# Decay attention and two feed-forward layers on one core: a fourth score tile in the late units' ring, and weight scales from column squares and products of ones

## The chip, the core and the metric

The kernel runs on one NeuronCore of a Trainium2 chip. The metric is the device time of one execution in microseconds (us). The core has five engines that run side by side and wait for each other through semaphores: TensorE (PE in the rows; its weight loads are PEld), VectorE (DVE), ScalarE (ACT), GpSimd (POOL) and SyncE (SP), whose queue issues the transfers here. Each takes its own instructions strictly in the order in which the program holds them.

## The reference

Attention with a decay, then two feed-forward layers over all 2304 tokens:

```
scores = q @ k.T / 8 + (cum[i] - cum[j]), causal      # 4 batches, 8 heads, 576 tokens, head size 64
x = softmax(scores) @ v                               # 2304 x 512
x = relu(x @ w_in) ** 2 @ w_out                       # 512 -> 2048 -> 512
g = x @ w_gate;  x = (silu(g) * (x @ w_val)) @ moe2_w_out   # 512 -> 1536 -> 512
```

`cum` is the running sum of log(f). Inputs and output are float32.

## The kernel before, in words

Most products are made three times in f16, with a high and a low part of each operand (hi*hi, hi*lo, lo*hi), so each f32 weight must be turned into two f16 tiles with a power-of-two scale, and that scale has to be known before the split.

**The plan.** The code doesn't issue instructions as it goes. Each piece of work is a step that `add` puts into a `Plan` with an engine, an estimated duration, the steps it depends on, the buffer rings it takes and uses, and a priority. `Plan.order` walks through time with these estimates, gives each free engine its ready step of the lowest priority number whose rings have room, and so fixes the order of every engine's instructions once and for all. On the chip an engine never passes over a step that is not ready. The tables of numbers at the top (`GPRI`, `EPRI`, `VPRI`, `IPRI`, `ILOAD`, `OPRI`, `OLOAD`, lines 167 to 173) are priorities of the early attention units, of V, and of the loads and steps of the weights.

**Fillers.** Exactly 130 steps `keep_clock` (line 295), each a 128x512 product of ones with itself into a bank that nobody reads, have the worst priority of all. The planner puts one wherever TensorE has nothing else that is ready and a bank of the ring `hp` is free; so where they stand in the order tells where the plan saw a hole on TensorE. All 130 are issued, in every case.

**Stages.** The attention is cut into 32 units: 16 early ones (tokens 0 to 255 of a batch and a pair of heads) and 16 late ones (tokens 256 to 575). `attn_unit` builds one. For each tile of 128 queries of a late unit TensorE makes the scores (line 817; for the 64 left-over tokens of both heads `tail_scores`, line 826, with the block tile `BOTH` that `corner` fills on POOL, line 767); DVE adds the decay into a score tile `s` (line 856), ACT takes the exponential (876) and the high part `p` (935), DVE the low part (939), SP transposes p by DMA (963), and TensorE mixes with V (`mix`, line 995). A late unit's Q is loaded to `qr` (722), rounded by ACT into the high part (737), and POOL makes the low part from both (740), which frees `qr`; `kr` likewise. Beside the attention TensorE works through the first feed-forward layer in token tiles of 256 (`mlp_pair`, lines 1193 and 1263); what is left of it follows the attention, and then comes the second layer in five rounds (`mlp2`, lines 1459 and 1575), each of which begins by finding a scale of its own input (line 1337 on TensorE).

**Scales of the weights.** `stage` loads a unit of 512 columns or rows of a weight in two or three pieces and joins the words; `extent` (line 417, DVE) takes the largest magnitude of each of the 128 partitions, one column of the table `MT` for each piece. `scale_of` calls `top`: TensorE turns the columns against an identity (line 326, `turn`), DVE takes the largest along the row (330) and squares it (332), TensorE spreads it with a product of ones (335, `spread`), and DVE makes the power of two (`power`, lines 305 to 311). Units 1 and 2 of gate and value are looked at early: `peek` loads them once for the extent alone (1078, 1084), ACT rescales (1099), and DVE shifts (1103) and copies into `MT` (1104); then the same `scale_of`. The four units of W_in take their extent from a Gram product instead.

Of the kernel before, what the change touches and what calls it, by code (L numbers as in the profile page):

```python
# [8 lines left out]
F32 = mybir.dt.float32  # L9
F32R = mybir.dt.float32r  # L10
F16 = mybir.dt.float16
BF16 = mybir.dt.bfloat16
I32 = mybir.dt.int32
# [150 lines left out]
    return 0.1 + n * 0.0021  # L164


GPRI = 866
GATE0 = -1
GATE = 5
EPRI = [394, 178, 220, -430, -80, -72, -882, -468, 406, -704, 233, 411, 552, 339, -276, -947]  # L170
VPRI = [84, 242, 446, 595]
IPRI, ILOAD = [-317, 915, 396, 320], [-195, 548, 99, 663]
OPRI, OLOAD = [368, 413, 378, 287], [27, -1147, 442, -1239]
VERBOSE = False
WHOLE = 2
SQUARE = 7
# [7 lines left out]
def decay_attention_moe_kernel(ctx: ExitStack, tc, q, k, v, f, w1, w2, wg, wv, wo, outT):  # L184
# [61 lines left out]
    XI, XS = table("xi", B + 1), table("xs", B + 1)  # L246
    KX = table("kx", 2, B * NP)
    FY = table("fy", B + 1)
    MT = table("mt", 2 * NG1 + 9 * NG2 + 4 * NG1, dt=BF16)
    NSC = 2 * NG1 + 3 * NG2  # L250
    SWI, SWS = table("swi", NSC), table("sws", NSC)
    ISF, ISG, ISV = (SWI[:, 2 * NG1 + NG2 * n : 2 * NG1 + NG2 * n + NG2] for n in range(3))
# [67 lines left out]
    def top(col, n, deps, pri, then, us, square=False, where="hp"):  # L320
        c = {}
        buf, alloc = bank(where)

        def turn():
            c["ps"] = alloc()
            nc.tensor.matmul(c["ps"][0:n, 0:P], col(), ident, start=True, stop=True)

        def largest():
            c["r"] = r = small.tile([P, 1], BF16, tag="top", bufs=4, name="top")
            nc.vector.tensor_reduce(r[0:n], c["ps"][0:n, 0:P], axis=mybir.AxisListType.X, op=ALU.max)  # L330
            if square:
                nc.vector.tensor_tensor(r[0:n], r[0:n], r[0:n], op=ALU.mult)

        def spread():
            nc.tensor.matmul(c["ps"][:, P : P + 1], ones[0:n, :], c["r"][0:n], start=True, stop=True)

        a = add(PE, 0.25, turn, [*deps, ready0], pri, take=[buf])
        r_buf = Buf("top", 4)
        a = add(DVE, 0.3 + (0.17 if square else 0), largest, [a], pri, take=[r_buf], use=[buf])
        a = add(PE, 0.15, spread, [a], pri, use=[buf, r_buf])  # L340
        return add(DVE, us, lambda: then(c["ps"][:, P : P + 1]), [a], pri, use=[buf])
# [17 lines left out]
    def stage(nm, u, places, pri, lpri, deps=(), gates=(), where="hp"):  # L359
# [55 lines left out]

        def extent(piece, at):
            nc.vector.tensor_reduce(
                MT[:, at : at + 1], piece["hi"].bitcast(F32), axis=mybir.AxisListType.X, op=ALU.max,
                apply_absolute_value=True,
            )  # L420

# [19 lines left out]
    def scale_of(nm, u, c, pri, where="hp"):  # L441
        idx = COL[nm] + u
        kk, mask = (13, 0x7F000000) if nm == "o" else (13 if nm in "gv" else 14, 0x7F800000)
        lo, hi = c["cols"]
        whole = 1 if nm == "i" else 512
        return top(
            lambda: MT[:, lo:hi], hi - lo, c["stat"], pri,
            lambda ps: power(ps, VSCALE * 1.02 * whole, kk, SWI[:, idx : idx + 1], SWS[:, idx : idx + 1], mask), 0.9,
            where=where, square=whole > 1,
        )  # L450

    def split(c, idx, slot, scaled):
        key, pri = c["key"], c["pri"]
# [226 lines left out]
    def attn_unit(idx, b, pr, half, opened):  # L680
# [34 lines left out]
        def raw_tile(name, w):  # L715
            if early:
                return h0.tile([P, SPLIT], F32, tag="qk", bufs=QKN, name=name)
            return pools["at"].tile([P, w], F32, tag=name, bufs=2, name=name)

        def load_q():  # L720
            c["qr"] = raw_tile("qr", QW)[:, :qn]
# [24 lines left out]
        def k_lo():  # L746
            nc.gpsimd.tensor_tensor(c["K"][:, 1], c["kr"], c["K"][:, 0].bitcast(F32), op=ALU.subtract)

        kr, qr = (Buf("qk", QKN), Buf("qk", QKN)) if early else (Buf("kr", 2), Buf("qr", 2))
        bias = kq_buf("bias")  # L750
        KA, QA = (kr, qr) if early else (kq_buf("KA"), kq_buf("Q"))
        lk = take(SP, DMA_ISSUE, load_k, [], [kr], nbytes=P * 4 * kmax)
# [3 lines left out]
        if not early:  # L756
            kh = take(ACT, act_us(kmax), k_hi, [lk], [KA], use=[kr])
            kl = add(POOL, pool_us(kmax), k_lo, [kh], pri, use=[KA, kr])
            qh = take(ACT, act_us(qn), q_hi, [lq], [QA], use=[qr])
            ql = add(POOL, pool_us(qn), q_lo, [qh], pri, use=[QA, qr])  # L760
            ready = [kh, kl, qh, ql]
            both = Buf("both%d" % (idx % 2), 1)

            def corner(h):
                def copy():
                    r = slice(64 * h, 64 * h + 64)
                    nc.gpsimd.tensor_copy(BOTH[idx % 2][r, :, r], c["Q"][r, :, QW - 64 : QW])

                return copy

            b0 = take(POOL, 0.44, corner(0), [qh, ql], [both], use=[QA])
            b1 = add(POOL, 0.44, corner(1), [qh, ql], pri, use=[QA, both], order=[b0])
            tail_ready = [kh, kl, b0, b1]
# [8 lines left out]
        for ti, i in enumerate(tiles):  # L782
# [9 lines left out]
            ng = heads[1][5] + 1  # L792
            cuts = [(0, ext if early else max(ext, 256))] if ext <= 512 else [(0, ext // 2), (ext // 2, ext)]
            cg_buf = Buf("cg", 6)
            sbufs = [Buf(tg + "s", SN if early else 3) for _ in range(ng)]
            masks = []
            for h, r0, r1, qc, M, g in heads:

# [9 lines left out]
            for ci, (n0, n1) in enumerate(cuts):  # L808
# [13 lines left out]
                def tail_scores(cuts=cuts, ti=ti):  # L822
                    for cc, (m0, m1) in enumerate(cuts):
                        c["ps", ti, cc, 0] = c["ps", ti, cc, 1] = at_tile()
                        for qi, ki in ((0, 0), (0, 1), (1, 0)):
                            nc.tensor.matmul(
                                c["ps", ti, cc, 0][:, : m1 - m0], BOTH[idx % 2][:, qi], c["K"][:, ki, m0:m1],
                                start=(qi, ki) == (0, 0), stop=qi == 1,
                            )

# [15 lines left out]
                for (h, r0, r1, _, _, g), mk, pbuf in zip(heads, masks, pbufs):  # L846
                    new = ci == 0 and (h == 0 or g == 1)

                    def soft(st=st, g=g, h=h, r0=r0, r1=r1, n0=n0, n1=n1, ti=ti, ci=ci, ext=ext, new=new):
                        if new:  # L850
                            st["s", g] = pool().tile([P, kw], F32, tag="s", bufs=SN if early else 3, name="s")
                            if g == 0:
                                st["cg"] = small.tile([P, 2, 4], F32, tag="cg", bufs=6, name="cg")
                        s, cg = st["s", g], st["cg"][:, g]
                        e1 = min(n1, ext)
                        nc.vector.tensor_tensor_reduce(  # L856
                            out=s[r0:r1, n0:e1], in0=c["ps", ti, ci, h][r0:r1, : e1 - n0],
                            in1=c["bias"][r0:r1, h, n0:e1],
                            scale=-0.125, scalar=3.0e38 if ci == 0 else cg[r0:r1, 0:1],
                            op0=ALU.add, op1=ALU.min, accum_out=cg[r0:r1, ci : ci + 1],  # L860
                        )
# [206 lines left out]
    def peek(nm, u, places):  # L1068
# [31 lines left out]

        def shift():
            t = cell["t"][:, : len(places)].bitcast(I32)
            nc.vector.tensor_scalar(t, t, 3, None, op0=ALU.logical_shift_left)
            nc.vector.tensor_copy(MT[:, m0 : m0 + len(places)], cell["t"][:, : len(places)])

        a = add(ACT, 0.3, real, [stats[-1][0]], GPRI, use=[t_buf])
        a = add(DVE, 0.35, shift, [a], GPRI, use=[t_buf])
# [539 lines left out]
    def open_half():  # L1647
# [4 lines left out]
        for n in range(2):  # L1652
# [123 lines left out]
```

## Time and profile before

| | before |
|---|---|
| median of 3 runs | 956.47 us (956.20 to 956.74) |
| the profiled execution | 959.76 us |
| its span, first to last instruction | 958.1 us |
| busy: PE, PEld | 944.1, 738.1 us |
| busy: DVE, ACT, POOL | 627.6, 603.4, 326.7 us |
| DMA | 117.46 MB, mean 123 GB/s |

The page cuts the span into 40 slices of some 24 us each. TensorE's digit is 9 in all of them but two 8s, the granted clock's likewise, the 18th slice (from 407 to 431 us) being one of the lower ones. DVE and ACT are at 7 to 9 tenths up to about the 24th slice (575 us) and at 3 to 4 tenths after it. A busy time is a share of the span, not a limit: TensorE's matmuls overlap and their ends are modelled, so how long one takes is read from the start of one to the start of the next.

### The profile page before, as it was taken

To read this page: it belongs to the slowest core of one execution; us is meant where nothing else is said; L and a number is where in the kernel's file an instruction comes from. 1 tells how busy PE (TensorE), PEld (TensorE's weight loads), DVE (VectorE), ACT (ScalarE), POOL (GpSimd) and SP (SyncE) were. 2 spreads that over 40 slices of the span, in tenths; PEclk is the share of its full clock that TensorE was granted. 3 is DMA by queue.
4 is the path that set the end of the run, shared out by engine and by line. 5 is a ranking of instruction groups with operands and counts; after the bars stand their busy time and mean duration, and the time that the engine had idled before them with its cause. 6 is when DMAs were issued, how large, how long until landed. Compare 5 with 4: busy or idle time off the path is not lost.

```text
span 958.1 us, 22457 instructions
## 1 busy us (share of the span) xinstructions
PE 944.1 (99%) x8845; PEld 738.1 (77%) x8845; DVE 627.6 (66%) x1438; ACT 603.4 (63%) x1147; POOL 326.7 (34%) x454
## 2 busy tenths in 40 slices
PE   9999999999999999989999999999999999999998
PEld 3686787888888788867888887778977776877774
DVE  4788888577666878768999898446464363433332
ACT  5899898588787898767978766225343343332332
POOL 1432163545544456333333453131321241110120
PEclk9999999999999999989999999999999999999999
DMA  9797249767979897999835411002020001000101
GB/s 286 229 360 243 42 113 216 224 164 149 182 150 191 176 230 182 241 220 269 204 111 175 156 45 45 2 1 90 1 66 2 2 1 44 2 1 12 34 1 44
DMA packets 147946, 117.46 MB, mean 123 GB/s; under 512 B 98241, under 2 KB 136129, under 8 KB 142593
## 3 DMA queue, kind: packets, MB, share of 16 engines
q1 hardware_dynamic: 147840, 116.04, 47.4%
q8 instruction: 69, 1.13, 0.5%
q14 instruction: 37, 0.29, 0.1%
HBM read 83.44 MB, written 9.51 MB: 97 GB/s over the span
## 4 chain that ended last, share of the span: by engine, by line
PE 51%; DVE 2%; issue 0%; ACT 0%; DMA 0%; SPq 0%; DVEq 0%; ACTq 0%
PE acc L1575 14%; PE v L1459 14%; PE h L1459 10%; PE acc L1263 6%; PE h L1193 5%; PE ps L995 1%; DVE r L1476 0%; PE ps L817 0%; DVE s L856 0%; DVE ms L1329 0%; DMA out_dram<-tmp 0%; DVE p L939 0%; DVE tmp L1476 0%; ACT L1497 0%; DVE i L1402 0%
## 5 line engine op out<-in xcount | busy, mean ns | idle before, releaser
L1193 PE MATMUL h<-x,i 128*128 128x256 f16 x1728 | 208.2, 274 | 0.0
L1263 PE MATMUL acc<-g,o 128*128 128x256 f16 x1728 | 207.6, 273 | 0.0
L1193 PEld LDWEIGHTS <-i 128*128 128x128 f16 x1728 | 164.8, 98 | 28.2 <-issue 6.3
L1263 PEld LDWEIGHTS <-o 128*128 128x128 f16 x1728 | 163.8, 98 | 28.1 <-issue 6.5
L1575 PE MATMUL acc<-o,f 128*128 128x512 f16 (+1 forms) x720 | 145.9, 358 | 0.9 <-ACT o L1548 0.5
L1575 PEld LDWEIGHTS <-f 128*128 128x128 f16 x720 | 70.0, 98 | 65.0 <-issue 1.4
L1538 POOL TENSOR_TENSOR tmp<-tmp,o 128x256 f32<-128x256 f32 (+1 forms) x30 | 23.4, 780 | 250.8 <-ACT o L1532 250.8
L1241 POOL TENSOR_TENSOR g<-tmp,g 128x512 f16<-128x512 f32 x56 | 71.5, 1276 | 106.9 <-ACT g L1236 94.9
L801 POOL TENSOR_SCALAR_AFFINE_SELECT bias<-bias 128x128 f32<-128x128 f32 (+1 forms) x160 | 61.6, 394 | 113.6 <-DVE cg L856 62.5
L939 DVE SCALAR_TENSOR_TENSOR p<-s,cg,p 128x512 f16<-128x512 f32 (+4 forms) x112 | 77.0, 702 | 27.7 <-ACT p L935 27.3
L876 ACT ACTIVATE s<-s,cg 128x256 f32<-128x256 f32 (+4 forms) x144 | 83.1, 579 | 17.8 <-DVE cg L856 17.6
L856 DVE CUSTOM_DVE_ANT_0 s<-ps,bias 128x512 f32<-128x512 f32 (+3 forms) x160 | 72.5, 479 | 24.3 <-PE ps L817 16.3
L935 ACT ACTIVATE p<-s,cg 128x512 f16<-128x512 f32 (+4 forms) x112 | 67.7, 615 | 7.7 <-issue 2.5
L1459 PEld LDWEIGHTS <-g 128*128 128x128 f16 x720 | 65.4, 98 | 8.8 <-issue 0.8
L1459 PEld LDWEIGHTS <-v 128*128 128x128 f16 x720 | 65.4, 98 | 6.5
L1504 ACT ACTIVATE r<-r,ms 128x768 f32<-128x768 f32 (+1 forms) x30 | 26.1, 869 | 69.8 <-DVE r L1476 69.7
L1459 PE MATMUL v<-i,g 128*128 128x256 f16 (+1 forms) x540 | 67.9, 262 | 0.4 <-DVE tmp L1476 0.4
L1459 PE MATMUL v<-i,v 128*128 128x256 f16 (+1 forms) x540 | 67.9, 262 | 0.0
L1476 DVE TENSOR_TENSOR r<-r,h 128x512 f32<-128x512 f32 (+1 forms) x30 | 19.0, 633 | 73.9 <-PE h L1459 67.0
L1542 POOL TENSOR_TENSOR r<-r,o 128x768 f32<-128x768 f32 (+1 forms) x30 | 45.8, 1526 | 41.3 <-ACT o L1535 40.5
L1476 DVE TENSOR_TENSOR r<-r,v 128x512 f32<-128x512 f32 (+1 forms) x60 | 38.0, 634 | 32.8 <-PE v L1459 30.6
L1459 PEld LDWEIGHTS <-eg 128*128 128x128 f16 x540 | 49.2, 98 | 8.9
(190 smaller groups left out, 1630.7 us busy)
## 6 DMA issues: line engine op xcount, KB each, us to landing
raw<-in_moe_w_out_dram SPq DMA_DIRECT2D x11, 1024.0 KB, 6.7
bias<-cum_d SPq DMA_DIRECT2D x16, 576.0 KB, 4.9
raw<-in_moe_w_val_dram SPq DMA_DIRECT2D x9, 1024.0 KB, 6.1
raw<-in_moe_w_gate_dram SPq DMA_DIRECT2D x9, 1024.0 KB, 6.8
raw<-in_moe_w_in_dram SPq DMA_DIRECT2D x8, 1024.0 KB, 5.8
vr<-in_v_dram SPq DMA_DIRECT2D x32, 256.0 KB, 4.3
x_d<-tmp SPq DMA_DIRECT2D x18, 256.0 KB, 3.6
kr<-in_k_dram SPq DMA_DIRECT2D x16, 288.0 KB, 4.1
```

The lines of the kernel that those rows point to most:

```text
L801: nc.gpsimd.affine_select(diag, diag, pattern=[[-1, w]], compare_op=ALU.is_ge, fill=-8e9, base=0, channel_multiplier=1)
L856: nc.vector.tensor_tensor_reduce(out=s[r0:r1, n0:e1], in0=c["ps", ti, ci, h][r0:r1, : e1 - n0], in1=c["bias"][r0:r1, h, n0:e1], scale=-0.1 ...
L876: nc.scalar.activation(s[:, :ext], s[:, :ext], AF.Exp, bias=cg[:, mc : mc + 1], scale=-1.0, accum_out=cg[:, 2:3],)
L935: nc.scalar.activation(pv[:, 0, :ext], s[:, :ext], AF.Copy, scale=cg[:, 3:4])
L939: nc.vector.scalar_tensor_tensor(pv[:, 1, :ext], s[:, :ext], cg[:, 3:4], pv[:, 0, :ext], op0=ALU.mult, op1=ALU.subtract,)
L1193: nc.tensor.matmul(HP[key][:, u, :], w[:, wi, kk, c * P : (c + 1) * P], x[:, xi, kk, :], start=(kk == 0 and (wi, xi) == (0, 0)), stop=(kk ...
L1241: lows[2].tensor_tensor(G[k0][1][:, 1], G[k0][0], G[k0][1][:, 0], op=ALU.subtract)
L1263: nc.tensor.matmul(acc[:, d - part[0], :], w[:, wi, c, d * P : (d + 1) * P], G[k0][1][:, gi, u, :], start=(m == 0 and d == part[0] and (wi ...
L1459: nc.tensor.matmul(R[reg][:, which, :w], t[:, wh, w1_ : w1_ + P], x[:, xh, xi, kk], start=fresh and which == 0 and kk == 0 and (wh, xh) == ...
L1476: nc.vector.tensor_tensor(out(), x(), y(), op=ALU.add)
L1542: nc.gpsimd.tensor_tensor(g, g, R["g"][:, 0, 1:4], op=ALU.subtract)
L1575: nc.tensor.matmul(acc_of(d), wd[:, cc, d * P : (d + 1) * P], R["g"][:, gi, 2 * m : 2 * m + 2].rearrange("p a t -> p (a t)"), start=mm == ...
```

## The change

It does four things. The 13 units of W_out, the second layer's output weight, gate and value no longer turn their extents: DVE squares each column of them (new line 458, one instruction for each piece), and TensorE multiplies each square with ones and sums them in one bank (new line 463); the extents stand in a float32 table `ME`, so `peek` needs one shift (1121) and no copy. W_in and V keep `top`. The late units' ring of score tiles has four tiles for three; in exchange `qr` has one buffer for two and `BOTH` one for two. And the tables of priorities have new numbers, which gives every engine another order.

```
-GPRI = 866
+GPRI = 864
-EPRI = [394, 178, 220, -430, -80, -72, -882, -468, 406, -704, 233, 411, 552, 339, -276, -947]
-VPRI = [84, 242, 446, 595]
-IPRI, ILOAD = [-317, 915, 396, 320], [-195, 548, 99, 663]
-OPRI, OLOAD = [368, 413, 378, 287], [27, -1147, 442, -1239]
+EPRI = [244, -200, -7, -648, 65, -536, 142, -686, 364, 99, 136, 548, 546, -423, -309, -1418]
+VPRI = [228, 246, 473, 561]
+IPRI, ILOAD = [-407, 890, 363, 306], [-509, 265, 885, 1236]
+OPRI, OLOAD = [402, 434, 247, 170], [-1221, -130, 84, -1046]
...
-    MT = table("mt", 2 * NG1 + 9 * NG2 + 4 * NG1, dt=BF16)
+    MT, ME = table("mt", NG1, dt=BF16), table("me", 2 * NG1 + 9 * NG2 + 4 * NG1)
...
-        whole = 1 if nm == "i" else 512
-        return top(
-            lambda: MT[:, lo:hi], hi - lo, c["stat"], pri,
-            lambda ps: power(ps, VSCALE * 1.02 * whole, kk, SWI[:, idx : idx + 1], SWS[:, idx : idx + 1], mask), 0.9,
-            where=where, square=whole > 1,
-        )
+        def then(ps, rows=1):
+            power(ps, VSCALE * 1.02 * rows, kk, SWI[:, idx : idx + 1], SWS[:, idx : idx + 1], mask)
+
+        if nm == "i":
+            return top(lambda: MT[:, lo:hi], hi - lo, c["stat"], pri, then, 0.9, where=where)
+        buf, alloc = bank(where)
+        r_buf, t = Buf("top", 4), {}
+
+        def squares():
+            t["r"] = r = small.tile([P, 4], BF16, tag="top", bufs=4, name="top")
+            for n in range(lo, hi):
+                m = ME[:, n : n + 1]
+                nc.vector.tensor_scalar(r[:, n - lo : n - lo + 1], m, m, None, op0=ALU.mult)
+
+        def total():
+            t["ps"] = alloc()
+            for n in range(hi - lo):
+                nc.tensor.matmul(t["ps"][:, 0:1], ones, t["r"][:, n : n + 1], start=n == 0, stop=n == hi - lo - 1)
+
+        a = add(DVE, 0.16 * (hi - lo), squares, c["stat"], pri, take=[r_buf])
+        a = add(PE, 0.1 + 0.06 * (hi - lo), total, [a, ready0], pri, take=[buf], use=[r_buf])
+        return add(DVE, 0.72, lambda: then(t["ps"][:, 0:1], 2), [a], pri, use=[buf])
...
-            return pools["at"].tile([P, w], F32, tag=name, bufs=2, name=name)
+            return pools["at"].tile([P, w], F32, tag=name, bufs=2 if name == "kr" else 1, name=name)
...
-            both = Buf("both%d" % (idx % 2), 1)
+            both = Buf("both%d" % (idx % 1), 1)
...
-            sbufs = [Buf(tg + "s", SN if early else 3) for _ in range(ng)]
+            sbufs = [Buf(tg + "s", SN if early else 4) for _ in range(ng)]
...
-            nc.vector.tensor_scalar(t, t, 3, None, op0=ALU.logical_shift_left)
-            nc.vector.tensor_copy(MT[:, m0 : m0 + len(places)], cell["t"][:, : len(places)])
+            m = ME[:, m0 : m0 + len(places)].bitcast(I32)
+            nc.vector.tensor_scalar(m, t, 3, None, op0=ALU.logical_shift_left)
```

What the order of the instructions shows, at three places. In the changed kernel line numbers above 445 are 17 higher.

TensorE, late in the attention, where the second of the four units that are looked at early (gate, unit 1) gets its scale: before, nine fillers stand between two score steps, and the turn follows at once.

```order
L817 MATMUL ps<-KA,Q 128x384 x6
L295 LDWEIGHTS ones
L295 MATMUL ps<-ones 128x512
...
L826 MATMUL ps<-KA,both 128x288 x6
L326 LDWEIGHTS mt
L326 MATMUL ps<-ident,mt 2x128
L995 LDWEIGHTS VT
```

The same place now; the scale's two products stand after a mix and before a full group of the first layer, and another such group comes before the next score step.

```order
L1012 MATMUL ps<-PT,VT 64x128
L463 LDWEIGHTS ones
L463 MATMUL ps<-top,ones 128x1
L463 LDWEIGHTS ones
L463 MATMUL ps<-top,ones 128x1
L1280 LDWEIGHTS o_1905
L1280 MATMUL acc<-g,o_1905 128x256
...
L834 MATMUL ps<-KA,Q 128x512 x6
```

The nine fillers are gone from here, and no filler stands anywhere in the late attention; up to this place there are 120 of them for 121.

DVE at the same scale, before: between the copy for the turn (1104) and the reduction of the turned row (330) stand ten instructions of the attention.

```order
L1103 TENSOR_SCALAR pk<-pk 128x2
L1104 CAST mt<-pk 128x2
L856 ISA s,cg<-ps,bias 64x288
...
L889 RECIPROCAL cg<-cg 128x2
...
L1025 SCALAR_TENSOR_TENSOR x<-ps,kx,x 128x128
L330 TENSOR_REDUCE top<-ps 2x1
L332 TENSOR_TENSOR top<-top 2x1
```

DVE there now:

```order
L873 ISA s,cg<-ps,bias,cg 64x288
L873 ISA cg 64x1
L1121 TENSOR_SCALAR me<-pk 128x2
L458 TENSOR_SCALAR top<-me 128x1 x2
L956 SCALAR_TENSOR_TENSOR p_7262<-s,cg,p_7262 128x384
```

Shift and squares follow each other, and TensorE waits for DVE once for a scale where it waited twice.

TensorE in the second layer, at the end of the round of the 64-token rests, and at the very end of the program, now; before, no filler stands at either place. Without the fillers, the last 2982 products of the program stand in the same order in both kernels.

```order
L1592 MATMUL acc<-o_11217,f_6520 128x256
L295 LDWEIGHTS ones
L295 MATMUL ps<-ones 128x512
...
L1592 MATMUL acc<-o_11433,f_5649 128x512
L295 LDWEIGHTS ones
L295 MATMUL ps<-ones 128x512
...
L1592 MATMUL acc<-o_13730,f_6520 128x512
L295 LDWEIGHTS ones
L295 MATMUL ps<-ones 128x512
L1789 UNCONDITIONAL_BRANCH
```

Two fillers stand at the first of these spots, five at the second (six products later), and three behind the last product of the program.

## Rows read from the trace of the kernel before

**Rows 1.** Busy time by stretch: span us, busy us (instructions) by engine, clock, DMA, GB/s.
```profile
core 0: us, PE busy (x) PEld busy (x) DVE busy (x) ACT busy (x) POOL busy (x), PEclk, DMA share, GB/s
...
408.40:415.20 6.80, 4.75 (x45) 3.07 (x46) 5.39 (x15) 3.01 (x10) 3.17 (x4) 1.00 1.16 156
415.20:422.00 6.80, 5.44 (x51) 3.40 (x50) 5.40 (x18) 3.59 (x7) 1.47 (x6) 0.50 1.00 320
...
490.00:690.00 200.00, 199.83 (x1940) 168.09 (x1938) 143.17 (x225) 116.46 (x178) 67.35 (x55) 1.00 0.19 62
...
720.00:953.00 233.00, 233.00 (x1730) 168.96 (x1728) 90.18 (x137) 76.58 (x125) 46.15 (x37) 1.00 0.03 11
```

**Rows 2.** Waits of TensorE, whole span: total us, times, longest.
```profile
PE ps L335 <- DVE top L332: 2.5, 4, 1.4
PE ps L326 <- DVE mt L1104: 2.1, 1, 2.1
```

**Rows 3.** TensorE in order of time, 408.9 to 422.6 us: start, duration, what, wait.
```profile
408.97 2.12 PE L295 MATMUL ps<-ones 128*128 128x512 bf16 x9
410.74 1.15 PE L826 MATMUL ps<-KA,both 128*128 128x288 f32 x6
413.95 0.22 PE L326 MATMUL ps<-ident,mt 128*2 128x128 bf16 x1 [2.06 <-DVE mt L1104]
414.09 0.69 PE L995 MATMUL ps<-PT,VT 128*64 128x128 f16 x18
414.72 1.02 PE L1193 MATMUL h<-x,i 128*128 128x256 f16 x6
417.10 0.16 PE L335 MATMUL ps<-top,ones 2*128 2x1 bf16 x1 [1.36 <-DVE top L332]
417.19 1.46 PE L1193 MATMUL h<-x,i 128*128 128x256 f16 x6
```

**Rows 4.** DVE in order of time, the same place.
```profile
409.68 1.22 DVE L1084 TENSOR_REDUCE pk<-raw 128x1 f32<-128x1024 f32 x1 [1.95 <-DMA raw<-in_moe_w_gate_dram]
...
413.72 0.17 DVE L1104 CAST mt<-pk 128x2 bf16<-128x2 f32 x1
...
416.59 0.27 DVE L330 TENSOR_REDUCE top<-ps 2x1 bf16<-2x128 f32 x1
416.90 0.15 DVE L332 TENSOR_TENSOR top<-top 2x1 bf16<-2x1 bf16 x1
```

**Rows 5.** TensorE in order of time: a 4-column product of ones, and what follows.
```profile
546.18 0.17 PE L1337 MATMUL ps<-sq,ones 128*128 128x4 bf16 x1
546.21 1.47 PE L1263 MATMUL acc<-g,o 128*128 128x256 f16 x12
```

**Rows 6.** TensorE in order of time where the second layer's third round begins to accumulate.
```profile
710.58 1.24 PE L1575 MATMUL acc<-o,f 128*128 128x512 f16 x5 [0.48 <-ACT o L1548]
712.22 1.46 PE L1575 MATMUL acc<-o,f 128*128 128x512 f16 x6 [0.39 <-DVE tmp L1606]
```

**Rows 7.** The program's end, in order of time: last products, last eviction.
```profile
952.23 1.46 PE L1575 MATMUL acc<-o,f 128*128 128x512 f16 x6
...
954.36 0.48 DVE L1606 TENSOR_SCALAR o<-acc,ms 128x256 f32<-128x256 f32 x1 [2.41 <-ACT o L1604]
```

**Rows 8.** Loads of Q (line 722): issue to landing; POOL frees a buffer; ACT's next cast.
```profile
DMA to landing us min/median/max: 2.1/3.4/9.3
...
361.36 0.87 POOL L740 TENSOR_TENSOR Q<-qr,Q 128x320 fp32r<-128x320 f32 x1
...
373.92 0.45 ACT L737 CAST Q<-qr 128x320 fp32r<-128x320 f32 x1
```

**Rows 9.** Loads of the peeks (line 1078): issue to landing; the DMA queue, 300 to 480 us.
```profile
DMA to landing us min/median/max: 5.8/6.9/8.5
...
q1 hardware_dynamic: 60023, 38.61, 94.1%
```

**Rows 10.** Busy time by stretch (columns as in rows 1), where weights are split.
```profile
500.00:550.00 50.00, 50.00 (x461) 44.83 (x459) 47.05 (x53) 40.87 (x50) 19.87 (x14) 1.00 0.48 159
550.00:600.00 50.00, 49.83 (x435) 42.19 (x434) 44.64 (x66) 32.04 (x48) 23.85 (x17) 1.00 0.14 43
```

More of the change, by code (lines that the diff above doesn't have):

```diff
@@ L328, in largest @@
         def largest():
-            c["r"] = r = small.tile([P, 1], BF16, tag="top", bufs=4, name="top")
+            c["r"] = r = small.tile([P, 4], BF16, tag="top", bufs=4, name="top")[:, 0:1]
             nc.vector.tensor_reduce(r[0:n], c["ps"][0:n, 0:P], axis=mybir.AxisListType.X, op=ALU.max)
@@ L417, in extent @@
             nc.vector.tensor_reduce(
-                MT[:, at : at + 1], piece["hi"].bitcast(F32), axis=mybir.AxisListType.X, op=ALU.max,
+                ME[:, at : at + 1], piece["hi"].bitcast(F32), axis=mybir.AxisListType.X, op=ALU.max,
                 apply_absolute_value=True,
@@ L747, in k_lo @@
             nc.gpsimd.tensor_tensor(c["K"][:, 1], c["kr"], c["K"][:, 0].bitcast(F32), op=ALU.subtract)
-        kr, qr = (Buf("qk", QKN), Buf("qk", QKN)) if early else (Buf("kr", 2), Buf("qr", 2))
+        kr, qr = (Buf("qk", QKN), Buf("qk", QKN)) if early else (Buf("kr", 2), Buf("qr", 1))
         bias = kq_buf("bias")
@@ L766, in copy @@
                     r = slice(64 * h, 64 * h + 64)
-                    nc.gpsimd.tensor_copy(BOTH[idx % 2][r, :, r], c["Q"][r, :, QW - 64 : QW])
+                    nc.gpsimd.tensor_copy(BOTH[idx % 1][r, :, r], c["Q"][r, :, QW - 64 : QW])
                 return copy
@@ L826, in tail_scores @@
                             nc.tensor.matmul(
-                                c["ps", ti, cc, 0][:, : m1 - m0], BOTH[idx % 2][:, qi], c["K"][:, ki, m0:m1],
+                                c["ps", ti, cc, 0][:, : m1 - m0], BOTH[idx % 1][:, qi], c["K"][:, ki, m0:m1],
                                 start=(qi, ki) == (0, 0), stop=qi == 1,
@@ L850, in soft @@
                         if new:
-                            st["s", g] = pool().tile([P, kw], F32, tag="s", bufs=SN if early else 3, name="s")
+                            st["s", g] = pool().tile([P, kw], F32, tag="s", bufs=SN if early else 4, name="s")
                             if g == 0:
@@ L1102, in shift @@
             t = cell["t"][:, : len(places)].bitcast(I32)
-            nc.vector.tensor_scalar(t, t, 3, None, op0=ALU.logical_shift_left)
-            nc.vector.tensor_copy(MT[:, m0 : m0 + len(places)], cell["t"][:, : len(places)])
+            m = ME[:, m0 : m0 + len(places)].bitcast(I32)
+            nc.vector.tensor_scalar(m, t, 3, None, op0=ALU.logical_shift_left)
         a = add(ACT, 0.3, real, [stats[-1][0]], GPRI, use=[t_buf])
-        a = add(DVE, 0.35, shift, [a], GPRI, use=[t_buf])
+        a = add(DVE, 0.2, shift, [a], GPRI, use=[t_buf])
         sc = PEEKED[nm, u] = scale_of(nm, u, {"cols": (m0, m0 + len(places)), "stat": [a]}, GPRI)
@@ L1651, in open_half @@
         )
-        for n in range(2):
+        for n in range(1):
             BOTH[n] = pools["at"].tile([P, 2, P], F32R, tag=f"both{n}", name="both")
```

## Prediction

> **What bounds the kernel now.** I read four views. First busy time by stretch [rows 1]: from 490 to 690 us TensorE is busy for 199.83 of 200 us and from 720 to 953 us for all of it, at full clock, so no other engine limits the second half, and only a shorter list of products or a hole that is filled can help there. What isn't full lies before 490 us. The worst place is 408.4 to 422.0 us: TensorE is busy for 4.75 and 5.44 us in two stretches of 6.8, and through the second the granted clock is 0.50, that is 1.2 GHz in place of 2.4.
>
> Second, TensorE's waits [rows 2]: 2.5 us in four waits at the spread (line 335) and 2.1 us in one at the turn (326). These are the scales of the weights, which the change rebuilds; no score product of the late units is in the list. Third, TensorE in order of time there [rows 3]: nine fillers, a tail score, then 2.06 us until the turn can start; soon after 1.36 us until the spread. Fourth, DVE at that place [rows 4]: it stood 1.95 us for a weight load, came to the copy for the turn only at 413.72, and to the square at 416.90; both times TensorE starts 0.2 us later. So DVE was late, and TensorE stood in its own fixed order behind it. With 94.1% of the DMA engines' time taken from 300 to 480 us, loads of the peeks take 5.8 to 8.5 us to land [rows 9].
>
> **The change, part by part.** Everything is summed against the profiled execution, 959.76 us, which is 3.29 us above the median of the runs.
>
> *Turns and spreads against products of ones.* 13 units lose a turn, 0.14 us to the next start (413.95 to 414.09), and a spread, 0.09 (417.10 to 417.19) [rows 3]: 13 x 0.23 = 3.0 us of TensorE. They gain 12 x 2 + 3 = 27 one-column products. The trace has none of those behind each other. From below: the 4-column product of ones takes 0.03 us from its start to the next [rows 5], but its weights could load under a long product ahead of it; from above: the spread's 0.09. I take 0.06, the middle, since the first of a pair is like the one and the second has no long product to hide its load: 27 x 0.06 = 1.6 us (0.8 to 2.4). Net **-1.4 us** (-2.2 to -0.6), all on the path, since TensorE is the bound. The Trainium skill (TensorE: Matmul & The Clock Gate, "Wait — 56ns, not 53.3ns?") gives small matmuls a floor of about 25 ns from start to start, and one of about 62 ns where the sequencer handles each; with the second the term would be -1.3 us, with the first -2.3, and no run here has yet shown which holds.
>
> *Fillers.* The nine at 408.97 take 1.77 us until the next start [rows 3], 0.20 each. The order has none there now, so in the plan the hole is filled with work of the first layer. Seven of them come back in the second layer: two ahead of a product that waits for 0.48 us today, five ahead of one that waits for 0.39 [rows 6]. The two (0.40) are hidden, the five (1.0) cost 0.6 us more than the wait. Three stand behind the last product, where the last eviction and the store run anyway: TensorE's last products start at 952.23, the last eviction at 954.36 [rows 7] and the span ends at 958.1; they cost nothing. Net -1.77 + 0.6 = **-1.2 us** (-1.8 if the waits cover all, 0 if the hole at 409 us stays as a wait).
>
> *Waits at the scales.* Of the 4.6 us [rows 2] most belongs to the units that change. Each of these now has one wait for DVE (the squares) where it had two, and shift, squares and products stand close together. But the products stand as close behind DVE's squares as the turn stood behind the copy, and DVE still takes the peeks' extents as soon as the plan thinks that they have landed. I let half go: **-2.3 us** (-4.3 to 0).
>
> *Clock.* It fell right after the two waits. From 417.19 to the stretch's end at 422.0 TensorE works 4.8 us at half clock [rows 1, 3], so six products of the first layer take 1.46 us there against 1.02 ahead of it, part of which already is at the low clock; at full clock the same work is half as long. If the holes shrink, the fall goes with them: **-2.4 us** (0 if it stays; a second fall elsewhere would cost as much again).
>
> *DVE.* It loses 13 x (0.27 + 0.15) and four copies of 0.17, 6.1 us [rows 4], and gains 27 squares, each about the 0.15 of the old one: 4.1. That is 2 us less on an engine that isn't the bound: 0 on the path, but some slack for the waits above.
>
> *Fourth score tile, single Q buffer, single BOTH.* No late score product waits today [rows 2], so the fourth tile by itself gives 0; what it does is let the planner place scores earlier. The single `qr`: POOL frees the buffer at 362.2 us and the next unit's cast is at 373.92 [rows 8], so 11.7 us are left for a load that lands in 3.4 us (9.3 at worst): 0. The single BOTH delays POOL's corner copies until the unit's own tail scores are done; the next tail scores come one unit, more than 10 us of products, later: 0. The Trainium skill (Trainium Kernel Development and Optimization, "Best Practices") says to double-buffer so that DMA overlaps compute, which speaks against the single `qr`; by it a load, 3.4 us, would stand ahead of every late unit. The 11.7 us of [rows 8] say that one buffer is early enough here.
>
> *The rest of the order* is new up to the first part of the second layer and the same after it. The time lost in small switches between kinds of products in the attention may move by a microsecond either way; I take 0.
>
> Sum: -1.4 - 1.2 - 2.3 - 2.4 = -7.3 us, 952.5 for an execution like the profiled one, **949.2 us** for the median.
>
> **The rivals.**
>
> (a) *The waits only move.* DVE stays late because the loads are (its 1.95 us stood for DMA, not for anything that the change touches), so each pair of products meets the wait that the spread met, and the clock falls all the same. For it: DMA is as full as before and the products stand right behind the squares. Against it: one wait for two, and no filler in the stretch. Then only products and fillers are left, -2.6 us: 953.9.
>
> (b) *DVE becomes the bound where gate and value are split.* From 500 to 600 us it is busy for 47.05 and 44.64 of 50 us [rows 10]. If TensorE gets there earlier, DVE may not, and the first products of the second layer wait for its splits. Then the gain shrinks to what DVE itself loses, 2.1 us: 954.4, about the edge of what can be told from no change. Against it: TensorE doesn't wait for any split there today.
>
> (c) *Slower: the load of Q comes too late.* With one buffer it can be issued only when POOL is through with the unit before, and it stands in SP's queue behind transpositions that wait for their own data. It decides when queue and landing together pass 11.7 us [rows 8]: at 9.3 us of landing, 2.4 us of waiting in the queue are enough. If the queue holds it by 5 us, each unit comes 2.6 us late; for half of the 16 units that is 21 us in the chain of the attention, of which TensorE can fill perhaps half with the first layer: +10.4 us on the forecast, 959.6. For it: DMA is almost full there. Against it: the median landing is 3.4 us, a third of what it would need.
>
> (d) *The new order is better still*: all the waits and the clock's fall go, the products cost 0.03 us, the waits of [rows 6] cover the fillers: -2.2 - 1.8 - 4.3 - 2.4 = -10.7, 945.8.
>
> **How the numbers follow.** The forecast has 0.52, (a) 0.19, (b) 0.13, (c) and other late chains that a wholly new order can hold 0.12, (d) 0.04. About 0.2%, 1.9 us, can be told from no change, so faster means under 954.6 and slower above 958.4. Faster: the forecast, (d), most of (a) and half of (b): 0.74. Same: the rest of (a) and (b), 0.14. Slower: (c), 0.12. The range goes from 945.0, just under (d), to 956.4, where (a) and (b) stand with their products at the upper price and nothing is left: some 0.17 lie above it and 0.03 below.
>
> **What would show it.** Right: no stretch of half clock after the first 50 us; the list of TensorE's waits has line 463 with 2 to 3 us in all and nothing longer than about 1 us; starts of paired one-column products lie some 0.06 us apart; the seven fillers leave no wait ahead of the two products of [rows 6]; the second half is as full as before, the same products some 7 us earlier. (a) would show waits of 1 us and more at line 463 and a clock of 0.50 near 410 us; (b) waits at the first products of line 1476 for DVE's line 563; (c) waits of TensorE or ACT for Q in the late units and idle time on ACT ahead of line 754 that a load ended. The forecast is wrong if the median lies above 954.6.

## The result, and the profile after

The changed kernel took 945.75 us (median of four runs, 944.63 to 946.94), the kernel before 956.61 on the same chip: a ratio of 0.9874, interval 0.9853 to 0.9895, or 10.9 us less. The forecast was 7.3 us less, and the range began at 945.0. The direction was right, the gain half as large again and close to the range's lower end. On another chip, where before takes 957.69 us, the ratio was 0.9859 (0.9833 to 0.9885; run after_again below).

The profiled execution took 944.63 us, its span is 942.8. TensorE's busy time in the stretches of [rows 1] (the first two at the same times, the last 15 us earlier), columns as there:

```profile
core 0: us, PE busy (x) PEld busy (x) DVE busy (x) ACT busy (x) POOL busy (x), PEclk, DMA share, GB/s
408.40:415.20 6.80, 6.80 (x79) 5.93 (x78) 2.83 (x7) 6.49 (x14) 3.06 (x3) 1.00 0.88 270
415.20:422.00 6.80, 6.80 (x75) 5.91 (x75) 6.62 (x15) 4.64 (x10) 4.35 (x8) 1.00 1.26 306
490.00:690.00 200.00, 199.77 (x1939) 167.98 (x1938) 135.70 (x225) 108.71 (x173) 71.05 (x56) 1.00 0.17 59
705.00:938.00 233.00, 233.00 (x1728) 168.79 (x1726) 89.93 (x137) 76.72 (x125) 45.75 (x37) 1.00 0.04 12
```

The two bad stretches are full and at full clock; the second half is as full as it was. All waits of TensorE, in the form of [rows 2]:

```profile
PE ps L295 <- POOL ones L279: 1.1, 1, 1.1
PE ps L409 <- DVE raw L388: 0.6, 1, 0.6
PE h L1210 <- ACT hold L1232: 0.6, 1, 0.6
PE ps L326 <- DVE mt L414: 0.5, 1, 0.5
PE ps L326 <- DVE pw L305: 0.3, 1, 0.3
PE v L1476 <- DVE tmp L1493: 0.2, 1, 0.2
```

Line 463, the new products of ones, isn't in it: no scale of the changed units holds TensorE up. The two places where units that are looked at early get their scale (before: [rows 3]), TensorE in order of time:

```profile
400.97 0.69 PE L1012 MATMUL ps<-PT,VT 128*64 128x128 f16 x18
401.59 0.20 PE L463 MATMUL ps<-top,ones 128*128 128x1 bf16 x2
401.66 0.81 PE L1280 MATMUL acc<-g,o 128*128 128x256 f16 x6
...
423.26 0.96 PE L834 MATMUL ps<-KA,Q 64*128 64x512 f32 x6
424.16 0.20 PE L463 MATMUL ps<-top,ones 128*128 128x1 bf16 x2
424.22 0.82 PE L1210 MATMUL h<-x,i 128*128 128x256 f16 x6
```

From the start of a pair to the start of the next product it is 0.06 to 0.07 us. Over all 27 products it is 0.95 us, 0.035 each: 19 of them take 25 to 29 ns, six 38 or 39, one 93 and one 121. I had taken 0.06 us each. The Trainium skill (TensorE: Matmul & The Clock Gate, "Wait — 56ns, not 53.3ns?") gives floors of about 25 and about 62 ns; here the first holds: none of the 27 takes less than 25 ns. DVE there (before: [rows 4]), in order of time:

```profile
400.62 0.43 DVE L1121 TENSOR_SCALAR me<-pk 128x2 int32<-128x2 int32 x1
401.08 0.34 DVE L458 TENSOR_SCALAR top<-me 128x1 bf16<-128x1 f32 x2
...
422.24 0.98 DVE L1121 TENSOR_SCALAR me<-pk 128x2 int32<-128x2 int32 x1
423.25 0.34 DVE L458 TENSOR_SCALAR top<-me 128x1 bf16<-128x1 f32 x2
```

The squares end at 401.42 and 423.59, and TensorE starts at 401.59 and 424.16: DVE is in time, by 0.2 and 0.6 us. The seven fillers in the second layer, where [rows 6] had two waits:

```profile
693.89 0.81 PE L295 MATMUL ps<-ones 128*128 128x512 bf16 x2
694.54 1.46 PE L1592 MATMUL acc<-o,f 128*128 128x512 f16 x6
695.83 1.25 PE L295 MATMUL ps<-ones 128*128 128x512 bf16 x5
696.91 1.46 PE L1592 MATMUL acc<-o,f 128*128 128x512 f16 x6
```

The waits are gone, and fillers of 0.65 and 1.08 us (start to next start) stand in their place.

### The profile page after: what moved, and what is told of

The parts are those of the page before. It is cut to its first block, busy times and chain, and to the rows that moved or that the text cites. A ratio compares the mean times of both kernels' runs of the same rounds, so it can differ in the third digit from the quotient of the medians.

```text
span 942.8 us, 22473 instructions
## 1 busy us (share of the span) xinstructions
PE 935.2 (99%) x8846; PEld 735.4 (78%) x8846; DVE 618.2 (66%) x1435; ACT 599.5 (64%) x1146; POOL 332.6 (35%) x454
## 4 chain that ended last, share of the span: by engine, by line
PE 94%; DMA 2%; DVE 2%; ACT 1%; issue 1%; POOL 0%; SPq 0%; POOLq 0%; DVEq 0%; ACTq 0%
PE acc L1280 21%; PE h L1210 19%; PE v L1476 15%; PE acc L1592 15%; PE h L1476 11%; PE ps L1012 4%; PE ps L834 4%; PE ps L295 3%; PE ps L843 1%; DMA raw<-in_moe_w_out_dram 1%; PE ps L927 1%; DMA bias<-cum_d 1%; PE ps L409 0%; DVE raw L388 0%; ACT o L485 0%
## 5 line engine op out<-in xcount | busy, mean ns | idle before, releaser
L1258 POOL TENSOR_TENSOR g<-tmp,g 128x512 f16<-128x512 f32 x56 | 74.9, 1338 | 90.4 <-ACT g L1253 84.0
L818 POOL TENSOR_SCALAR_AFFINE_SELECT bias<-bias 128x128 f32<-128x128 f32 (+1 forms) x160 | 63.5, 406 | 110.1 <-DMA bias<-cum_d 55.2
```

Of the source, the lines that this page charges most:

```text
L818: nc.gpsimd.affine_select(diag, diag, pattern=[[-1, w]], compare_op=ALU.is_ge, fill=-8e9, base=0, channel_multiplier=1)
L1258: lows[2].tensor_tensor(G[k0][1][:, 1], G[k0][0], G[k0][1][:, 0], op=ALU.subtract)
```

## The experiments

Ratios are to the kernel before on the same chip, with their interval; one per cent is 9.6 us.

**A second look at before.**

> The kernel before once more, for a second profile. If the execution shown ahead of the prediction is typical, the waits at lines 326 and 335 near 410 us and the clock of 0.50 after them are there again. If it was a long one (its 959.76 us stand 3.3 us above the median), the clock's fall or some of the waits is missing and the span is 954.5 to 955.5 us.

It is a single execution, 955.53 us, with a span of 953.8, on a chip where 23 others took 954.3 to 963.0. TensorE by stretch (only TensorE's columns), and in order of time:

```profile
core 0: us, PE busy (x), PEclk, DMA share, GB/s
405.00:425.00 20.00, 17.08 (x191) 1.00 1.17 240
```

```profile
407.54 2.12 PE L295 MATMUL ps<-ones 128*128 128x512 bf16 x9
409.31 1.14 PE L826 MATMUL ps<-KA,both 128*128 128x288 f32 x6
411.87 0.22 PE L326 MATMUL ps<-ident,mt 128*2 128x128 bf16 x1 [1.42 <-DVE mt L1104]
...
414.97 0.16 PE L335 MATMUL ps<-top,ones 2*128 2x1 bf16 x1 [1.50 <-DVE top L332]
```

The fillers and both waits are there again, the fall of the clock is not: the second case, with a span 0.7 us under what I gave for it. So the waits belong to the kernel, the fall to an execution. What the fall cost can be read from the two executions of the same program: their spans differ by 4.3 us, but the fillers start at 408.97 us in one [rows 3] and at 407.54 in the other, so 1.4 us were lost before the hole (the stretch of half clock near 20 us lasts 6.8 us in one and 3.4 in the other). The waits are 0.5 us longer in the first, 3.4 for 2.9 us, which leaves about 2.4 us for the clock.

Low clocks are common. Of 79 executions of before beside these experiments, the 32 with a mean granted clock of 0.997 or more took 956.9 us on average, the 21 with 0.996 took 958.8 and the 26 with 0.995 or less 961.1; the mean counts a low stretch wherever it lies, so it doesn't say which of these fell near 410 us. Of the changed kernel's ten executions none is below 0.996. Executions of 956.2 to 956.7 us, as in the median that I forecast from, are found only among those with 0.997 or more; the profiled one, 959.76, has 0.993. I take the pair with spans of 953.8 and 942.8 us for the sum below, since each has one stretch of half clock, 3.4 us near 20 us, and none later in its work; they are two single executions, but their difference, 11.0 us, is that of the medians, 10.9.

**The nine fillers alone.** The last nine are not issued, the order is kept:

```
     def keep_clock():
+        made.append(0)
+        if 121 < len(made) <= 130:
+            return
```

> The kernel before without the last nine fillers, the ones at 408.97 us, all else in the same order. Theory A (they fill a true hole): the wait at line 326 grows by 1.2 to 1.8 us, same time, 956 to 957. Rival (they cost what they take): 954.7, the wait stays at 2.1 us.

0.9984 (0.9970 to 0.9998). In its profile the wait for the copy grew from 1.42 to 4.24 us, by more than the 1.8 us of the fillers and more than I expected, and the wait at the spread shrank from 1.50 to 0.40:

```profile
407.28 1.06 PE L831 MATMUL ps<-KA,both 128*128 128x288 f32 x6
412.59 0.27 PE L331 MATMUL ps<-ident,mt 128*2 128x128 bf16 x1 [4.24 <-DVE mt L1109]
...
415.75 0.16 PE L340 MATMUL ps<-top,ones 2*128 2x1 bf16 x1 [0.40 <-DVE top L337]
```

The hole near 410 us is 4.6 us with the fillers left out and was 1.8 + 1.42 + 1.50 = 4.7 us with them. So they filled a true hole; leaving them out gives little or nothing.

**One part at a time, in the old order.** `inside` keeps before's plan; the new scales are made in the old steps:

```
         def turn():
             c["ps"] = alloc()
+            if cols: return
...
         def largest():
+            if cols:
+                for k in range(*cols):
+                    m = ME[:, k : k + 1]
+                    nc.vector.tensor_scalar(r[:, k - cols[0] : k - cols[0] + 1], m, m, None, op0=ALU.mult)
+                return
...
         def spread():
+            if cols:
+                for k in range(n):
+                    nc.tensor.matmul(c["ps"][:, P : P + 1], ones, c["r"][:, k : k + 1], start=k == 0, stop=k == n - 1)
+                return
```

> The kernel before with its own order and rings; only the scales are made in the new way, inside the old steps (the turn's step issues nothing, the squares stand where the reduction stood, the products of ones where the spread stood). Theory A (the late waits hang on where the order puts DVE's part and the loads; the new way itself is worth only its shorter list, 13 x 0.25 us less 27 x 0.035 us = 2.3 us): 953.0 to 955.0, line 335's place still waits 1.4 to 3.4 us near 410 us and the clock still falls there. Rival B (one wait in place of two does it, in any order): the waits and the clock's fall go as well, 947 to 950.

0.9951 (0.9934 to 0.9967), 4.7 us less: between theory and rival. The wait stays, once in place of twice:

```profile
413.24 0.28 PE L345 MATMUL ps<-top,ones 128*128 128x1 bf16 x2 [2.03 <-DVE top L335]
```

and the clock fell for 3.4 us after it. Rival B falls: one wait in place of two doesn't remove the hole in this order. But 4.7 us is twice what the shorter list gives by the starts (2.3); the part on what a turn costs says why.

`ring` has only the four score tiles, the single `qr` and the single `BOTH` (those three pieces of the change's diff), planned with the old tables. Its order is new as well, since the planner fills the larger ring.

> Before with the fourth score tile, single Q buffer and single BOTH alone, old tables, old scales. Theory A: 0 by itself, 955 to 958, waits at lines 326 and 335 as before. Rival C (the fourth tile lets scores run ahead and fills the holes): 948 to 952 and no filler in the late attention. Rival D (the single Q buffer costs): above 958.5, with TensorE or ACT waiting for Q.

0.9961 (0.9943 to 0.9979), 3.7 us less, some 952.8 us where before takes 956.5: my 0 falls, and rival C's 952 is nearly reached. One filler is left near there, at 406.05. DVE in order of time where, at about the same time, a unit that is looked at early gets its scale (401.27 is an extent of a peek; before, DVE stood 1.95 us ahead of one), with TensorE behind it:

```profile
401.27 1.23 DVE L1084 TENSOR_REDUCE pk<-raw 128x1 f32<-128x1024 f32 x1
...
405.95 0.21 DVE L1104 CAST mt<-pk 128x2 bf16<-128x2 f32 x1
```

```profile
407.02 0.22 PE L326 MATMUL ps<-ident,mt 128*2 128x128 bf16 x1
...
408.55 0.17 PE L335 MATMUL ps<-top,ones 2*128 2x1 bf16 x1
```

DVE no longer stands for a peek's load and is ahead; both waits near 410 us are gone, with the old scales. What goes with the larger ring shows in DVE's waits too: the time for which DVE stands for ACT's high part of p, over the whole span, in `before_again` and then in `ring` (total, times, longest):

```profile
DVE p L939 <- ACT p L935: 28.4, 31, 3.5
```

```profile
DVE p L939 <- ACT p L935: 16.6, 25, 1.4
```

In the changed kernel it is 16.0, in `ring_tables` and `ring_inside` below 16.8 and 17.5; in the runs with three tiles it is 20.0 to 31.4. But `scale_ring` has the fourth tile and 28.4, so the tile alone doesn't do it, and how it leads to an order without the two waits is not shown. This order has a price as well: TensorE stands 1.92 us for DVE's line 1476 at the second layer's first products, at 573.67 us. The time lies under rival D's 958.5, and neither TensorE nor ACT waits for a load of Q, so rival D falls.

`ring_inside` puts the new scales into the steps of that order.

> The fourth score tile with single Q buffer and BOTH, old tables, in the order that the run ring had, and the new scales inside the old steps of that order (as in the run inside). Theory A (the two gains are of different kinds, a shorter list of products and fewer waits near 410 us, and add up): 0.9951 x 0.9961, a ratio of 0.9912, some 948 us where before is 956.5; the new tables would then be worth the rest of the change, 3 to 4 us. Rival (both remove the same waits): a ratio of 0.994 to 0.995.

0.9913 (0.9884 to 0.9942), where the product of the two ratios is 0.9912. The parts add up. Some 8.3 us of the gain are theirs; the new tables and the order planned from them give the rest, 0.9859 to 0.9874 against 0.9913, that is 3.7 to 5.2 us, and less sure than the parts, since each interval is 0.2 to 0.3% wide to either side. Where the rest lies shows in the waits that this order still has between 200 and 600 us, a scale's among them:

```profile
406.14 0.28 PE L345 MATMUL ps<-top,ones 128*128 128x1 bf16 x2 [1.37 <-DVE top L335]
...
569.56 0.82 PE L1471 MATMUL v<-i,g 128*128 128x256 f16 x6 [1.90 <-DVE tmp L1488]
```

The clock didn't fall after the first of them. The changed kernel has no wait in that stretch, so these 3.3 us are most of the rest.

**What a turn costs.** `turn128` is before with 128 columns in each turn of a weight's extents:

```
-            lambda: MT[:, lo:hi], hi - lo, c["stat"], pri,
+            lambda: MT[:, lo : lo + P], hi - lo, c["stat"], pri,
```

> The kernel before with the same order; each turn of a weight's extents takes 128 columns of the table in place of its 1 to 4 (the others are zeros or other units' extents, and their rows of the result are not read). Theory A (a turn is dear because its 128x2 weights differ in shape from the 128x128 ones before and after it: 0.15 us for itself and 0.09 us on the product ahead of it): each turn takes 0.06 us, the product ahead of it is no longer than others of its kind, 0.15 to 0.2 us less for each of some 15 turns, a ratio of 0.997. Rival (it is dear as an operation that loads new weights under 128 columns): 0.15 us and the 0.09 us ahead stay, a ratio of 1.000.

One turn between two products of the first layer, in order of time: in `before_again`, then in `turn128`.

```profile
388.20 1.47 PE L1263 MATMUL acc<-g,o 128*128 128x256 f16 x12
389.61 0.22 PE L326 MATMUL ps<-ident,mt 128*2 128x128 bf16 x1
389.76 1.48 PE L1263 MATMUL acc<-g,o 128*128 128x256 f16 x12
```

```profile
390.18 1.47 PE L1265 MATMUL acc<-g,o 128*128 128x256 f16 x12
391.49 0.22 PE L328 MATMUL ps<-ident,mt 128*128 128x128 bf16 x1
391.55 1.47 PE L1265 MATMUL acc<-g,o 128*128 128x256 f16 x12
```

The same twelve products take 1.41 us to the turn's start, then 1.31; the turn itself 0.15, then 0.06. So it is in each turn of a weight's extents that follows a 128*128 product without a wait. It is the shape, 128*2 between 128*128, that costs 0.09 us ahead of the turn and 0.09 in it; the operation does not. The Trainium skill (TensorEngine Tiling (Array Packing), "Key Properties") says that a change of tiling mode drains TensorE. The trace shows 0.09 us at such a change; that it is the drain it does not show, and the page gives no price. The spread, with 2 to 4 rows of weights, has the same 0.096 us on the product ahead in eight cases past 100 us, and takes 0.105 itself; ahead of a product of ones with a 128*128 product in front there is nothing. So a unit's turn and spread cost up to 0.09 + 0.15 + 0.10 + 0.105 = 0.45 us. In `before_again` the 13 units' turns and spreads take 3.2 us to the next starts. The extra on the product ahead is there for 8 of the 13 turns and 8 of the 13 spreads, 1.5 us in all; the others follow a wait, another turn, or a product of another shape. Less 0.95 for the new products that makes 3.7 us, inside the interval of `inside` (3.2 to 6.3 us). The time of `turn128` itself, 0.9988 (0.9969 to 1.0008), does not tell the 0.9970 expected from 1.

`after_wide` gives the eight turns and spreads that the changed kernel kept (W_in, V) the full shape:

```
+    MV = table("mv", B * NP + NG1 + P, dt=BF16)
+    vmax, MT, ident = MV[:, : B * NP], MV[:, B * NP : B * NP + NG1], MV[:, B * NP + NG1 :]
...
-            lambda: vmax[:, n0 : n0 + NP], NP,
+            lambda: MV[:, n0 : n0 + P], NP,
...
+            m = FIRST[:, 0:1] if n == 1 else FIRST[:, 1:2]
+            nc.vector.tensor_scalar(r, r, m, None, op0=ALU.mult)
...
-            nc.tensor.matmul(c["ps"][:, P : P + 1], ones[0:n, :], c["r"][0:n], start=True, stop=True)
+            nc.tensor.matmul(c["ps"][:, P : P + 1], ones, c["r"], start=True, stop=True)
```

> The changed kernel, same order, with the eight turns and spreads that it kept (W_in and V) given 128x128 weights as well: the turn takes 128 columns (the unit's, then others and the identity), DVE multiplies the largest by 1 or 0 for each partition, and the spread takes all of ones. Theory A (the shape is what is dear): each turn 0.056 us and each spread 0.03 us with nothing on the product ahead, 8 x (0.20 + 0.17) = 3 us less where nothing waits; some half of these stand at waits for DVE that stay, so a ratio of 0.9845 to 0.986 and 943.5 to 945 us. Rival (DVE's extra instruction lengthens the chain of the early scales): as the changed kernel or slower, 0.987 to 0.989.

0.9874 (0.9845 to 0.9903): no gain that the interval shows, and its middle lies in the rival's range, not in the theory's. Some of these scales stand where TensorE waits for the engine ahead of it:

```profile
61.26 0.28 PE L331 MATMUL ps<-mv 128*128 128x128 bf16 x2 [1.10 <-DVE mv L421]
63.95 0.37 PE L1217 MATMUL h<-x,i 128*128 128x256 f16 x1 [2.41 <-ACT hold L1239]
```

The changed kernel waits 0.5 and 0.6 us at these two, so what the products save there is lost again in waits. This execution is the slowest of six (951.24 us, median 946.62) and has its half clock there, from 62.55 us; whether DVE's extra instruction lengthens the waits, as the rival has it, stays open.

**The plan and its numbers.** Five kernels that mix the parts and let the planner order them anew: `scale` and `tables` have one part each, `scale_ring` and `ring_tables` two, and `s3` is the changed kernel with three score tiles:

```
-            sbufs = [Buf(tg + "s", SN if early else 4) for _ in range(ng)]
+            sbufs = [Buf(tg + "s", SN if early else 3) for _ in range(ng)]
```

> Before with the new scales alone, planned anew with the old tables and the ring of three. Theory A: the products' 2.3 us and at most 1 us of waits, 952.5 to 955. Rival B (the new scales carry the change): 946 to 949.5. Rival C (the fourth score tile carries it): 954 to 956.

> Before with the new tables of priorities alone. Theory A (the numbers fit the new scales and the new ring, and are of no use without them): 955 to 960. Rival E (the tables alone place the loads and DVE's part of the scales better, and carry the change): 946 to 951, late waits at lines 326 and 335 gone.

> The changed kernel with three score tiles in the late ring (Q buffer and BOTH stay single), planned anew. Theory A (scales and order carry the change): 945 to 949. Rival C (the fourth tile carries it): 951 to 956, fillers or waits in the late attention.

> The changed kernel with the old tables of priorities: new scales and the fourth score tile, planned anew. Theory A (the numbers have to fit the plan; the parts are worth 0.9913 in the old order, but the plan with old numbers falls into a bad order as it did with the scales alone): a ratio of 1.000 to 1.015. Rival (the fourth tile gives the plan room, so the old numbers do): 0.989 to 0.993.

> The changed kernel with the old scales: new tables and the fourth score tile, planned anew. Theory A (numbers tuned for another list of steps): a ratio of 1.000 to 1.015. Rival (ring and tables belong together, the scales only shorten the list by 4 to 5 us): 0.990 to 0.993.

| | ratio | interval |
|---|---|---|
| new scales alone | 1.0174 | 1.0146 to 1.0202 |
| new tables alone | 1.0172 | 1.0146 to 1.0197 |
| scales and ring | 1.0086 | 1.0059 to 1.0113 |
| ring and tables | 1.0040 | 1.0023 to 1.0058 |
| scales and tables, single `qr` and `BOTH` (`s3`) | 1.0018 | 1.0003 to 1.0032 |
| all three | 0.9874, 0.9859 | 0.9853 to 0.9895, 0.9833 to 0.9885 |

`scale_ring` and `ring_tables` came as the theory had it; in the other three I was wrong. I expected 952.5 to 955 us of `scale` and it took 974.3, 955 to 960 of `tables` and it took 973.8, and `s3`, where I thought that scales and order carry the change, took 961.1, above its rival's 956 too: with these tables the fourth tile has to be there. The same scales that save 4.7 us in the old order lose 17 when the planner may move everything else for them. In `scale` and `s3` the largest losses lie where before had its hole; the longest waits of TensorE in `scale`, then in `s3`:

```profile
PE ps L463 <- DVE top L458: 5.9, 2, 3.4
PE ps L843 <- DVE x L1042: 3.1, 2, 2.6
```

```profile
PE ps L1012 <- DMA PT<-p: 4.1, 1, 4.1
PE h L1210 <- DVE x L1042: 2.2, 1, 2.2
```

From 400 to 450 us TensorE is busy for 39.40 of 50 us in `scale`, with a granted clock of 0.76, and for 41.19 in `s3`, with 0.90; in `ring` and in the changed kernel for all 50. In `s3` ten fillers stand between 401.67 and 405.73, ahead of the wait for the transposition. In `tables` TensorE is busy there as in before (46.30 of 50 us), and its longest wait, 4.4 us, is at the start of the second layer. `ring_tables` is full from 400 to 450 us, `scale_ring` busy for 47.85; both wait at the start of the second layer, in `scale_ring` 3.15 and 3.00 us:

```profile
569.63 1.44 PE L1476 MATMUL h<-i,g 128*128 128x256 f16 x6 [3.15 <-ACT r L1503]
...
575.35 0.81 PE L1476 MATMUL v<-i,g 128*128 128x256 f16 x6 [3.00 <-DVE tmp L1493]
```

So rival E falls as well: the tables alone cost 1.7%. Which number of the tables does what was not tried.

**The changed kernel again, and without its last ten fillers.**

> The changed kernel once more, on the chip of the two runs beside it. A ratio of 0.986 to 0.989, waits of 0.2 us and less at line 463.

0.9859 (0.9833 to 0.9885), no wait at line 463.

> The changed kernel without its last ten fillers (seven in the second layer, three behind the last product), all else in the same order. Theory A (they cost 0.6 us more than the two waits that they cover): 945.1, that is 0.6 us under the changed kernel, and the waits of 0.48 and 0.39 us come back ahead of the same two products. Rival (the waits grow to cover all of it): 945.7, no difference. Rival (they keep the clock up): slower, a stretch of 0.50 near 710 us.

0.9852 (0.9833 to 0.9870) on another chip; with the edit of before_no9 at 120. The waits came back, the second of them longer:

```profile
697.67 1.24 PE L1597 MATMUL acc<-o,f 128*128 128x512 f16 x5 [0.48 <-ACT o L1570]
699.65 1.46 PE L1597 MATMUL acc<-o,f 128*128 128x512 f16 x6 [0.74 <-DVE tmp L1628]
```

A gain of 0.6 us is too small for these intervals, and the clock didn't fall there. Here line 463 waited once for 0.59 us, at 427.00: its margin is thin. No version beat the changed kernel by more than the intervals.

## Why the prediction was wrong

The sum once more, for the pair of spans 953.8 and 942.8:

| term | forecast | measured | from |
|---|---|---|---|
| turns and spreads against products | -1.4 | -3.7 | 3.2 in their own starts, 1.5 in the products ahead of them, less 0.95 for the products of ones |
| late waits at the scales | -2.3 | -3.8 | 0.43 + 1.42 + 1.50 + 0.47, none left |
| clock | -2.4 | 0 | same early fall in both, no late one |
| fillers | -1.2 | -1.3 | nine gone, 1.8; 0.65 + 1.08 for two waits that cost 0.65 + 0.56 with their restart |
| all else | 0 | -2.2 | the rest, by subtraction: early waits some 0.4, restarts behind the late waits some 0.5, the others not found |
| sum | -7.3 | -11.0 | |

Two steps failed, one in the mechanism and one in a size; a third error, the clock, hid a part of both.

*Fourth tile and waits: the mechanism.* "No late score product waits today [rows 2], so the fourth tile by itself gives 0" was read from TensorE's waits alone, and the waits at the scales were put down to the new way of making them. The runs show the reverse. The ring alone gives 3.7 us, and both waits near 410 us go with the old scales; the new scales alone, in the old order, keep a wait of 2.03 us and a fall of the clock there. With both (`ring_inside`) 1.37 us came back, and only the order from the new tables has none. So the late waits went by the order that the ring and the tables allow, and not by half. By which step the fourth tile leads to such an order stays open.

*Turns and spreads: the size.* I read the price of a turn and a spread from their start to the next start (0.14 and 0.09), at a place where TensorE had waited for both, and so missed what they do to the product ahead of them: 0.09 to 0.10 us in 16 of 26 cases, 1.5 us. And I took 0.06 us for a product of ones, "the middle"; it is 0.035, near my lower bound. Together 2.3 us too little.

*Clock.* Its price was right, about 2.4 us in an execution that has the fall. But I forecast the median, whose executions by their times don't have it, by a subtraction of 3.29 us that already held the fall: it was counted twice. So the forecast was 2.4 us too good here, and without this error it would have been -4.9 against -11.0. Nor did the clock fall "right after the two waits": it is low through the whole stretch from 415.20 us [rows 1], and the second wait ends at 417.10 [rows 3].

*Fillers* came as forecast: the hole was true, the seven cost about half a microsecond more than their waits, the three at the end nothing.

*Rivals.* (a) fell for the whole change: DVE still stood twice for a peek's load, 2.1 and 1.9 us (line 1101 in its waits), and no unit's scale waited for it. For the new scales alone, in `inside`, it came true near 410 us. (b) fell here, TensorE waits 0.2 us at line 1476; `scale_ring` has waits of 3 us at that line, but for ACT's line 1503 and DVE's 1493, not for the splits of line 563. (c) fell: Q lands after 2.2, 4.2 and 8.5 us (least, median, most), and no engine waits for it with one buffer. (d), 945.8, which I gave 0.04, is nearest: it had the products at 0.03 and all the waits gone. That its time is right is luck in part: it missed the products ahead of the turns and the rest, and counted the clock, which about cancel.

## To carry to other kernels

The price of a small matmul is not its own start-to-start time: look at the product ahead of it. Weights of the full shape (128*128) in a stream of such products were cheaper here even where most columns were waste; the rows show it, while the times of `turn128` and `after_wide` are too close to call. A list of TensorE's waits doesn't tell what a larger buffer is worth where a planner makes the order from it: look at the waits of the engine that fills the buffer too, and measure. Try an edit inside the old order first: the same edit gave 0.9951 there and 1.0174 planned anew, and the tables that belong to the change cost 1.7% without the rest of it.

## What the runs showed of the hardware

A product of ones with one column, with its own load of 128x128 weights each time, starts 25 to 29 ns ahead of the next product in 19 of 27 cases; a product with 2 columns of weights behind a 128*128 one costs 0.09 us on that product, and takes 0.15 us itself where one with 128 columns takes 0.06. The granted clock fell to 0.50 at the hole near 410 us in some executions of the same program and not in others: with waits of 2.06 and 1.36 us in the execution shown ahead of the prediction, not with 1.42 and 1.50 in `before_again`, and with 1.42 and 1.49 in `turn128`, whose order is the same. So the length of the waits alone doesn't decide it here.
